# Forgetting attention with an MLP on one core: the first batch's decay columns, its attention, its waits and its loads put in another order

## The chip, the core and the metric

The kernel runs on one core of one Trainium2 chip. The metric is the device time of one execution in microseconds (us); three runs of the kernel before gave 365.26, 366.35 and 366.67 us, a median of 366.35 us.

## What is computed

There are 8 batches of 8 heads, 576 positions and 64 dimensions. Each head's scores are q·k/8, plus a decay: the difference of the running sums of log f at the two positions. Positions after one's own are masked. The attention output, 4608 rows of 512, goes through an MLP without biases.

```python
scores = scale * np.matmul(q, k.transpose(0, 1, 3, 2))
log_f = np.log(np.clip(f, 0.0001, 1.0))
cum = np.cumsum(log_f, axis=-1)
decay = cum[:, :, :, None] - cum[:, :, None, :]
scores = np.where(causal, -1000000000.0, scores + decay)
attn = np.exp(scores - np.max(scores, axis=-1, keepdims=True))
x = (attn / (attn.sum(-1, keepdims=True) + 1e-9)) @ v     # then to (4608, 512)
h = x @ w_in                                              # 512 -> 2048
out = (h - np.tanh(h)) @ w_out                            # 2048 -> 512
```

## The kernel before

All engines run in the order in which the program emits their instructions (a manual schedule covers TensorE, VectorE, ScalarE, GpSimd and SyncE), so an instruction that waits holds up everything behind it on its own engine. The order of the first batch is written out by hand at the end of the function; from the second batch on, `slot(p, take)` goes through pairs of heads and mixes `take` MLP steps into each pair's attention.

**The decay** enters the score matmul as extra contraction rows: besides the 64 dimensions, the transposed q and k have three rows that hold the running sum of log f (scaled) in a high and a low half-precision part. For the first batch these values are written as *columns* D to D+2 of `qa` and `ka`, the untransposed q and k (five blocks of up to 128 positions), before TensorE transposes them. `decay_sum` (L148) makes the running sum `cum` in two pieces, positions 0 to 255 and 256 to 575. `decay_turn` (L166) turns it by TensorE into PSUM, and `decay_cols(ib)` (L175 to L178) writes block ib's columns with three VectorE instructions. For later batches the values come as *rows*: `decay_rows` (L152 to L155) writes `chi`, `cq` and `clo`, and `load_aug` (L143 to L145) copies a batch's rows with three DMAs of SyncE's queue.

**The first batch, block by block.** `trans0(ib, what, pool, eng)` (L267) makes eight TensorE transposes of q's or k's block ib; one VectorE copy (L272) or ScalarE copy (L270) takes them into `QT` or `KT`. `scores0(ib, ti)` (L282, mask matmuls L285) makes tile ti of the block's scores, and ScalarE's exp (L287) takes it into an `e` tile. The score tiles have two PSUM buffers. Blocks 0 to 4 have 2, 4, 6, 8 and 5 tiles, 25 in all. `values0(ib)` (L295) multiplies them with v into the PSUM tile `av`, of which there is one buffer; VectorE divides by the row sums (L300 to L302) and so reads `av` last. `turn0(ib)` (L311, copy L312) transposes the result into `XR`, the MLP's input.

**MLP steps.** `step()` emits the next entry of one long list: for each unit of 512 tokens 16 steps of `mlp1`, then 16 of `mlp2`. A step of the first unit (`mlp1` with u = 0, L396) is eight matmuls of 256 tokens: step s takes the token half s // 8 and the two hidden blocks 2 (s % 8) and 2 (s % 8) + 1. ScalarE's tanh (L384) and VectorE's add (L386) follow each step. The order by hand has eight steps in the first batch, and the second batch's four pairs take 4, 4, 3 and 3, all later ones 8.

**Spins.** `spin(n)` (L239) issues n matmuls of 512 columns that nobody reads, into a new tile of the same pool and tag as `av`.

**Loads.** GpSimd issues all loads of q, k, v, `w_in` and `w_out` in program order, as casting DMAs on one queue. In the opening these are blocks of batch 0 (`load_block` L86, 128 KB each as written), `w_in` in four quarters (`load_win` L182, 512 KB each), batch 1's q and k for heads 0 to 3 in four pieces (`load_qk` L190, 144 KB each), batch 1's v in five blocks, its q and k for heads 4 to 7 (288 KB each), and `w_out` in four quarters (L186). The four quarters of `w_in` stand between the blocks of q, k and v.

**Batch 1** starts with `trans(1, 0, ...)` of q and k (L250, copies L257 and L259) and then `scores` (L335, mask L338, exp L344) and `values` (L363) of pair 0 of batch 1.

Of the kernel before, what the change touches and what calls it, by code (L numbers as in the profile page):

```python
# [8 lines left out]
FP32 = mybir.dt.float32  # L9
FP16 = mybir.dt.float16  # L10
AF = mybir.ActivationFunctionType
ALU = mybir.AluOpType
# [10 lines left out]
def kernel(  # L23
# [10 lines left out]
    nc = tc.nc  # L34
    P = 128

    B, H, S, D = q.shape
# [46 lines left out]
    def load_block(dst, src, b, n, h0=0, h1=H):  # L84
        pn = min(P, S - n * P)
        nc.gpsimd.dma_start(out=dst[0:pn, n, h0:h1, 0:D], in_=src[b, h0:h1, n * P:n * P + pn, :].rearrange("h p d -> p h d"))  # L86

    def turn_block(dst, src, b, n):
        pn = min(P, S - n * P)
        nc.sync.dma_start_transpose(out=dst[:, :, n * P:n * P + pn], in_=src[b % 2][0:pn, n, :, :])  # L90
# [4 lines left out]
    def load_v(b, n):  # L95
        load_block(vn[b % 2], v, b, n)
# [20 lines left out]
    nc.vector.memset(ka[:, :, :, D + 2:D + 3], 1.0)  # L117
    nc.vector.memset(ones16, 1.0)
    nc.vector.memset(tri16, 0.0)
    load_block(qa, q, 0, 0)  # L120
    load_block(ka, k, 0, 0)
    nc.gpsimd.affine_select(out=id16, in_=id16, compare_op=ALU.not_equal,
                            fill=1.0, base=0, pattern=[[-1, P]], channel_multiplier=1)
    load_block(qa, q, 0, 1)
    load_block(ka, k, 0, 1)
    nc.gpsimd.affine_select(out=tri16, in_=tri16, compare_op=ALU.is_ge,
                            fill=BIG, base=0, pattern=[[1, P]], channel_multiplier=-1)
    nc.vector.memset(minus16, -1.0)
# [18 lines left out]
    def decay_sum(c0, c1):  # L147
        nc.vector.tensor_tensor_scan(out=cum[:, c0:c1], data0=ones16[0:NH, c0:c1], data1=lf[:, c0:c1],  # L148
                                     initial=cum[:, c0 - 1:c0] if c0 else 0.0, op0=ALU.mult, op1=ALU.add)

    def decay_rows():
        nc.vector.tensor_scalar_mul(out=chi, in0=cum, scalar1=inv_qscale)  # L152
        nc.vector.tensor_scalar(out=cq, in0=cum, scalar1=inv_qscale, scalar2=-SHIFT * inv_qscale,
                                op0=ALU.mult, op1=ALU.add)
        nc.vector.scalar_tensor_tensor(out=clo, in0=cum, scalar=inv_qscale, in1=chi,  # L155
                                       op0=ALU.mult, op1=ALU.subtract)

    CT = {}
    keep = cst.tile([P, NJ * H], FP32)

    def decay_turn(blocks):
        t32 = ps_tr.tile([P, UW], FP32, tag="tr", name="t32")
        for ib in blocks:
            pn = min(P, S - ib * P)
            CT[ib] = (keep if 2 in blocks else t32)[0:pn, ib * H:(ib + 1) * H]
            nc.tensor.transpose(out=t32[0:pn, ib * H:(ib + 1) * H], in_=cum[0:H, ib * P:ib * P + pn], identity=id32)  # L166
        if 2 in blocks:
            nc.vector.tensor_copy(out=keep[:, 2 * H:4 * H], in_=t32[:, 2 * H:4 * H])
            nc.vector.tensor_copy(out=keep[0:D, 4 * H:5 * H], in_=t32[0:D, 4 * H:5 * H])

    def decay_cols(ib):
        ct = CT.pop(ib)
        pn = min(P, S - ib * P)
        hi = ka[0:pn, ib, :, D]
        nc.vector.tensor_scalar(out=qa[0:pn, ib, :, D + 2], in0=ct, scalar1=inv_qscale,  # L175
                                scalar2=-SHIFT * inv_qscale, op0=ALU.mult, op1=ALU.add)
        nc.vector.tensor_scalar_mul(out=hi, in0=ct, scalar1=inv_qscale)
        nc.vector.scalar_tensor_tensor(out=ka[0:pn, ib, :, D + 1], in0=ct, scalar=inv_qscale, in1=hi,  # L178
                                       op0=ALU.mult, op1=ALU.subtract)

    def load_win(f0, f1):
        nc.gpsimd.dma_start(out=win[:, :, f0:f1],  # L182
                            in_=moe_w_in[:, f0:f1].rearrange("(c p) f -> p c f", p=P))
# [5 lines left out]
    def load_qk(dst, src, b, h0, h1):  # L189
        nc.gpsimd.dma_start(  # L190
            out=dst[b % 2][:, h0:h1, :, :].rearrange("p h n d -> p h (n d)"),
            in_=src[b, h0:h1, :, :].rearrange("h (p n) d -> p h (n d)", n=NT6))

    load_v(0, 0)
    load_v(0, 1)
    load_block(qa, q, 0, 2)
    load_block(ka, k, 0, 2)
    load_win(0, DFF // 4)
    load_v(0, 2)
    load_block(qa, q, 0, 3)  # L200
    load_block(ka, k, 0, 3)
    load_v(0, 3)
    load_win(DFF // 4, DFF // 2)
    load_block(qa, q, 0, 4)
    load_block(ka, k, 0, 4)
    load_v(0, 4)
    load_win(DFF // 2, 3 * DFF // 4)
    load_win(3 * DFF // 4, DFF)
    for h in (0, 2):
        load_qk(qn, q, 1, h, h + 2)  # L210
        load_qk(kn, k, 1, h, h + 2)
    nc.sync.dma_start(out=QT[1][D:D + 2, :, :], in_=minus16)
    nc.sync.dma_start(out=KT[1][D + 2:D + 3, :, 0:S], in_=ones16[0:H, :])

# [21 lines left out]
    def spin(n):  # L236
        av = ps_av.tile([P, 2, 512], FP32, tag="av", name="spin")
        for _ in range(n):
            nc.tensor.matmul(out=av[:, 0, :], lhsT=ones16[:, 0:P], rhs=ones16[:, 0:UW])  # L239
# [20 lines left out]

    def trans0(ib, what, pool, eng):
        src, dst = (qa, ka)[what], (QT, KT)[what][0]
        pn = min(P, S - ib * P)
        t32 = pool.tile([P, UW], FP32, tag="tr" if pool is ps_tr else "m", name="t32")
        t16 = t32.bitcast(FP16)[0:D + 3, 0:H * pn].rearrange("p (h n) -> p h n", h=H)
        for h in range(H):
            nc.tensor.transpose(out=t16[:, h, :], in_=src[0:pn, ib, h, 0:D + 3], identity=id16[0:pn, 0:pn])  # L267
        to = dst[:, :, ib * P:ib * P + pn]
        if eng == "A":
            nc.scalar.activation(out=to, in_=t16, func=AF.Copy)  # L270
        else:
            nc.vector.tensor_copy(out=to, in_=t16)  # L272
# [115 lines left out]

    def mlp1(u, s):
        if u == 0:  # L390
            t, fp = divmod(s, NFT // 2)
            hps = ps_m.tile([P, UW], FP32, tag="m", name="hps")
            for w in range(2):
                ft = 2 * fp + w
                for ci in range(NCH):
                    nc.tensor.matmul(out=hps[:, w * SB:(w + 1) * SB], lhsT=win[:, ci, ft * P:(ft + 1) * P],  # L396
                                     rhs=XR[:, ci, t * SB:(t + 1) * SB], start=(ci == 0), stop=(ci == NCH - 1))
            gt = gate(hps)
            for w in range(2):
                for m in range(2):  # L400
                    GT[(0, 2 * fp + w, 2 * t + m)] = gt[:, w * SB + m * P:w * SB + (m + 1) * P]
            return
        hps = ps_m.tile([P, UW], FP32, tag="m", name="hps")
        t0 = u * UW % RING
        parts = [(0, t0, min(UW, RING - t0))]
        if t0 + UW > RING:
            parts.append((RING - t0, 0, t0 + UW - RING))
        for o, t, n in parts:
            for ci in range(NCH):
                nc.tensor.matmul(out=hps[:, o:o + n], lhsT=win[:, ci, s * P:(s + 1) * P],  # L410
                                 rhs=XR[:, ci, t:t + n], start=(ci == 0), stop=(ci == NCH - 1))
        gt = gate(hps)
        for m in range(UW // P):
            GT[(u, s, m)] = gt[:, m * P:(m + 1) * P]
# [44 lines left out]
    def slot(p, take):  # L459
# [7 lines left out]
                given += 1  # L467
        step(take - given)

    spin(8)  # L470
    decay_sum(0, 2 * P)
    decay_turn((0, 1))
    decay_cols(0)
    trans0(0, 0, ps_m, "V")
    trans0(0, 1, ps_m, "A")
    spin(2)
    decay_cols(1)
    trans0(1, 0, ps_m, "V")
    scores0(0, 0)
    scores0(0, 1)  # L480
    trans0(1, 1, ps_tr, "V")
    decay_sum(2 * P, S)
    spin(2)
    decay_turn((2, 3, 4))
    scores0(1, 0)
    values0(0)
    scores0(1, 1)
    scores0(1, 2)
    decay_cols(2)
    trans0(2, 0, ps_m, "V")  # L490
    turn0(0)
    scores0(1, 3)
    trans0(2, 1, ps_tr, "V")
    scores0(2, 0)
    values0(1)
    scores0(2, 1)
    scores0(2, 2)
    turn0(1)
    decay_rows()
    load_aug(1)  # L500
    step()
    scores0(2, 3)
    step()
    scores0(2, 4)
    for e in EL:
        nc.vector.memset(e, 0.0)
    nc.vector.memset(KT[1][:, :, S:PITCH], 0.0)
# [5 lines left out]
    load_qk(kn, k, 1, HH, H)  # L513
    for t in range(0, NFT, 4):
        load_wout(t, t + 4)
    decay_cols(3)
    trans0(3, 0, ps_m, "V")
    trans0(3, 1, ps_tr, "V")
    scores0(2, 5)
    scores0(3, 0)  # L520
    values0(2)
    scores0(3, 1)
    step()
    scores0(3, 2)
    turn0(2)
    step()
    scores0(3, 3)
    decay_cols(4)
    trans0(4, 0, ps_m, "V")
    trans0(4, 1, ps_tr, "V")  # L530
    scores0(3, 4)
    scores0(3, 5)
    step()
    scores0(3, 6)
    step()
    scores0(3, 7)
    scores0(4, 0)
    values0(3)
    scores0(4, 1)
    scores0(4, 2)  # L540
    turn0(3)
    step()
    scores0(4, 3)
    trans(1, 0, qn, QT, "AV")
    step()
    scores0(4, 4)
    trans(1, 0, kn, KT, "VV")
    values0(4)
    TAKE = [4, 4, 3, 3, 8]
    for p in range(NPAIR, len(pairs) + 1):  # L550
        slot(p, TAKE[p - NPAIR] if p < NPAIR + len(TAKE) else 8)
        if p == NPAIR:
# [30 lines left out]
```

## Time and profile before

| | |
|---|---|
| median of three runs | 366.35 us (365.26 to 366.67) |
| the profiled execution | 364.9 us, of it 363.2 us between first and last instruction |
| TensorE | 346.0 us busy (95%) |
| ScalarE | 223.1 us busy (61%) |
| VectorE | 193.5 us busy (53%) |
| GpSimd | 151.2 us busy (42%) |
| first score matmul of batch 1 (L335) | 44.94 us |
| first step of `mlp2` (L422) | 60.16 us |

In the rows of the profile PE is TensorE, PEld its weight loads, DVE VectorE, ACT ScalarE, POOL GpSimd and SP SyncE; SPq or POOLq stand for an engine's sequencer. A row of the timeline has the start, the duration (from the start of the first to the end of the last of the merged instructions), engine, line, operation, what is written and read, shape and count, and in brackets the idle time of the engine before it with what ended it. Matmuls are pipelined: the next one starts before the last one has ended, so the cost of a group is read from start to start.

### The profile page before, as it was taken

The page shows a single profiled execution, that of the slowest core. Times are in us where ns is not written, and L with a number is a line of the kernel's source. Part 1 is how long each engine was busy: PE and PEld are TensorE (multiplying, and loading weights), DVE is VectorE, ACT ScalarE, POOL GpSimd, SP SyncE. Part 2 cuts the span into 40 slices and gives each one's busy share as a digit, 9 for nine tenths or more (in the row PEclk, how much of TensorE's full clock was granted, in tenths as well). Part 3 has the DMA queues.
Part 4 walks back from the last instruction along what each step waited for, and adds up shares of the span by engine and source line. Part 5 has one row for each costly group of instructions (what it writes and reads, how often), then busy time and mean ns, then how long its engine had stood idle before and what let it go on. Part 6 is the DMA issues. An engine that isn't in the chain of part 4 may idle for free.

```text
span 363.2 us, 7847 instructions
## 1 busy us (share of the span) xinstructions
PE 346.0 (95%) x2989; PEld 200.9 (55%) x2989; DVE 193.5 (53%) x366; ACT 223.1 (61%) x411; POOL 151.2 (42%) x290
## 2 busy tenths in 40 slices
PE   6768799999999999999999999999999999999995
PEld 3558687555555555555556875555555554444442
DVE  5675679547982378237832773277327612712810
ACT  5436597646765686568756875687558734713621
POOL 8766433066267636764576447642222210000000
PEclk9989999999999999999999999999999999999999
DMA  9999999599959995999699969992220022011002
GB/s 95 155 196 169 200 203 138 72 110 174 117 36 159 140 159 55 156 150 142 67 148 155 147 65 134 157 151 44 76 75 18 18 74 74 2 47 69 3 30 85
DMA packets 149495, 38.70 MB, mean 107 GB/s; under 512 B 137362, under 2 KB 144850, under 8 KB 149458
## 3 DMA queue, kind: packets, MB, share of 16 engines
q0 software_dynamic: 101184, 18.36, 71.5%
q1 hardware_dynamic: 48194, 19.77, 27.9%
q8 instruction: 23, 0.38, 0.5%
q14 instruction: 14, 0.11, 0.1%
q10 hardware_dynamic: 80, 0.08, 0.1%
HBM read 36.85 MB, written 9.44 MB: 127 GB/s over the span
## 4 chain that ended last, share of the span: by engine, by line
PE 89%; DVE 5%; ACT 2%; issue 1%; DMA 1%; POOL 0%; POOLq 0%; ACTq 0%
PE ops L422 34%; PE hps L410 30%; PE ps L335 10%; PE av L363 7%; PE hps L396 3%; DMA qn<-in_q_dram 1%; DVE gt L386 1%; ACT th L384 1%; PE ps L282 1%; PE t L267 1%; ACT e L344 1%; PE t L250 1%; PE av L295 1%; DVE KT L259 1%; DVE xn L302 1%
## 5 line engine op out<-in xcount | busy, mean ns | idle before, releaser
L422 PE MATMUL ops<-wout,gt 128*128 128x512 f16 x576 | 140.4, 378 | 0.0
L386 DVE TENSOR_TENSOR gt<-hps,th 128x512 f16<-128x512 f32 x144 | 99.1, 690 | 61.7 <-ACT th L384 61.0
L344 ACT ACTIVATE e<-ps 128x512 f16<-128x512 f32 x168 | 99.4, 594 | 49.5 <-PE ps L335 38.2
L410 PE MATMUL hps<-XR,win 128*128 128x512 f16 (+1 forms) x576 | 125.7, 355 | 0.2
L384 ACT ACTIVATE th<-hps 128x512 f32<-128x512 f32 x144 | 86.0, 597 | 30.2 <-PE hps L410 23.7
L354 POOL TENSOR_SCALAR_AFFINE_SELECT e<-e 128x128 f16<-128x128 f16 x144 | 48.8, 339 | 114.9 <-ACT e L344 114.0
L422 PEld LDWEIGHTS <-gt 128*128 128x128 f16 x576 | 51.8, 97 | 52.5
L410 PEld LDWEIGHTS <-win 128*128 128x128 f16 x576 | 52.3, 97 | 44.2 <-issue 0.5
L335 PE MATMUL ps<-QT,KT 67*128 67x512 f16 (+1 forms) x336 | 70.9, 277 | 2.5 <-DVE KT L259 1.6
L335 PEld LDWEIGHTS <-KT 67*128 67x128 f16 x336 | 32.8, 98 | 35.4 <-DVE KT L259 1.9
L426 ACT ACTIVATE ost<-ops 128x512 f32<-128x512 f32 x36 | 21.5, 597 | 38.3 <-PE ops L422 38.3
L369 DVE TENSOR_SCALAR rs<-av 128x10 f32<-128x10 f32 x28 | 4.6, 164 | 68.4 <-PE av L363 68.4
L86 POOL DMA_DIRECT2D vn<-in_v_dram x40 | 34.1, 854 | 11.3 <-DMA win<-in_moe_w_in_dram 4.5
L363 PEld LDWEIGHTS <-e 128*128 128x128 f16 x784 | 28.1, 97 | 5.5
L86 POOL DMA_DIRECT2D qn<-in_q_dram x30 | 25.8, 861 | 8.3 <-PE ps L338 2.7
L363 PE MATMUL av<-vn,e 128*128 128x65 f16 x784 | 29.1, 193 | 0.0
L86 POOL DMA_DIRECT2D kn<-in_k_dram x30 | 25.8, 858 | 0.8 <-issue 0.6
L371 DVE TENSOR_TENSOR xn<-av,rs 128x640 f16<-128x640 f32 x28 | 23.1, 825 | 1.0
L287 ACT ACTIVATE e<-ps 128x512 f16<-128x512 f32 x25 | 14.3, 596 | 12.0 <-PE ps L285 10.6
L396 PE MATMUL hps<-XR,win 128*128 128x256 f16 x128 | 16.6, 272 | 0.5 <-DVE XR L312 0.5
L259 DVE COPY QT<-t 64x576 f16<-64x576 f16 x12 | 9.7, 806 | 9.0 <-PE t L250 6.7
L259 DVE COPY KT<-t 64x576 f16<-64x576 f16 x16 | 12.7, 795 | 1.1 <-PE t L250 1.0
(81 smaller groups left out, 199.7 us busy)
## 6 DMA issues: line engine op xcount, KB each, us to landing
out_dram<-ost SPq DMA_DIRECT2D x36, 256.0 KB
vn<-in_v_dram POOLq DMA_DIRECT2D x32, 128.0 KB, 5.9
qn<-in_q_dram POOLq DMA_DIRECT2D x24, 128.0 KB, 4.4
kn<-in_k_dram POOLq DMA_DIRECT2D x24, 128.0 KB, 4.6
win<-in_moe_w_in_dram POOLq DMA_DIRECT2D x4, 512.0 KB, 9.1
wout<-in_moe_w_out_dram POOLq DMA_DIRECT2D x4, 512.0 KB, 12.6
XR<-xn SPq DMA_TRANSPOSE x56
qn<-in_q_dram POOLq DMA_DIRECT2D x1, 576.0 KB, 15.3
```

Of the source, the lines that this page charges most:

```text
L86: nc.gpsimd.dma_start(out=dst[0:pn, n, h0:h1, 0:D], in_=src[b, h0:h1, n * P:n * P + pn, :].rearrange("h p d -> p h d"))
L259: nc.vector.tensor_copy(out=to, in_=of)
L335: nc.tensor.matmul(out=ps[:, col:col + n], lhsT=KT[b % 2][0:D + 3, h, j * P:(j + 1) * P], rhs=QT[b % 2][0:D + 3, h, i0:i0 + n], start=True ...
L344: nc.scalar.activation(out=e[:, lo:hi], in_=ps[:, lo:hi], func=AF.Exp, scale=qscale)
L354: nc.gpsimd.affine_select(out=view, in_=view, compare_op=ALU.is_ge, fill=0.0, base=0, pattern=pat, channel_multiplier=-1)
L363: nc.tensor.matmul(out=av[:, a, ib, :], lhsT=E.pop((b, 2 * c + a, j, ib)), rhs=vn[b % 2][:, j, 2 * c + a, 0:D + 1], start=(j == 0), stop=( ...
L371: nc.vector.tensor_tensor(out=xn.rearrange("p i (a d) -> p a i d", a=2), in0=av[:, :, :, 0:D], in1=rs.to_broadcast([P, 2, NJ, D]), op=ALU. ...
L384: nc.scalar.activation(out=th, in_=hps, func=AF.Tanh, scale=-1.0)
L386: nc.vector.tensor_tensor(out=gt, in0=hps, in1=th, op=ALU.add)
L396: nc.tensor.matmul(out=hps[:, w * SB:(w + 1) * SB], lhsT=win[:, ci, ft * P:(ft + 1) * P], rhs=XR[:, ci, t * SB:(t + 1) * SB], start=(ci == ...
L410: nc.tensor.matmul(out=hps[:, o:o + n], lhsT=win[:, ci, s * P:(s + 1) * P], rhs=XR[:, ci, t:t + n], start=(ci == 0), stop=(ci == NCH - 1))
L422: nc.tensor.matmul(out=ops, lhsT=GT[(u, ft, m)], rhs=wout[:, ft, :], start=(ft == 0), stop=(ft == NFT - 1))
```

## The change

- The second piece of `decay_sum` comes right behind block 0's columns. `decay_turn` of blocks 2, 3 and 4 comes ahead of block 1's transposes, into the same PSUM tile as blocks 0 and 1, and `decay_cols(2, NJ)` writes the columns of blocks 2, 3 and 4 at once, three instructions in all. The tile `keep` and its two copies go.
- `decay_rows` is split in two and goes ahead with `load_aug(1)` to block 0's and 1's scores.
- Block 4 has 64 positions; `load_first` and `trans0` now place it in partitions 64 to 127.
- `w_in` is loaded in two halves instead of four quarters, and both go behind all of batch 0's blocks; the second also goes behind batch 1's first four pieces of q and k. The order of `mlp1` with u = 0 becomes: four steps of token half 0, four of token half 1 with the same hidden blocks, then the same for the other hidden blocks.
- The first batch's order has one MLP step after `scores0(4, 2)` and four more behind it: five in all instead of eight. The pairs from the second batch on take 4, 4, 3, 3, 10, 9 and then 8.
- Three more spins of one matmul each stand in blocks 1 and 2.

```diff
+    def load_first(dst, src, n):
+        p0 = max(0, (n + 1) * P - S)
+        nc.gpsimd.dma_start(out=dst[p0:P, n, :, 0:D],
+                            in_=src[0, :, n * P:(n + 1) * P - p0, :].rearrange("h p d -> p h d"))
...
     def decay_turn(blocks):
-        t32 = ps_tr.tile([P, UW], FP32, tag="tr", name="t32")
+        if not CT:
+            CT.append(ps_tr.tile([P, UW], FP32, tag="tr", name="ct"))
         for ib in blocks:
...
+            t0 = min(ib * P, S - P)
+            nc.tensor.transpose(out=CT[0][:, ib * H:(ib + 1) * H], in_=cum[0:H, t0:t0 + P], identity=id32)
-        if 2 in blocks:
-            nc.vector.tensor_copy(out=keep[:, 2 * H:4 * H], in_=t32[:, 2 * H:4 * H])
-            nc.vector.tensor_copy(out=keep[0:D, 4 * H:5 * H], in_=t32[0:D, 4 * H:5 * H])
...
-            t, fp = divmod(s, NFT // 2)
+            t, fp = s // 4 % 2, s // 8 * 4 + s % 4
...
+    load_v(0, 0)
     spin(8)
     decay_sum(0, 2 * P)
     decay_turn((0, 1))
-    decay_cols(0)
+    decay_cols(0, 1)
+    decay_sum(2 * P, S)
     trans0(0, 0, ps_m, "V")
     trans0(0, 1, ps_m, "A")
+    decay_turn((2, 3, 4))
+    decay_cols(2, NJ)
+    load_first(qa, q, 2)
+    load_first(ka, k, 2)
+    load_v(0, 1)
+    load_first(qa, q, 3)
+    load_first(ka, k, 3)
+    load_v(0, 2)
+    load_v(0, 3)
+    load_first(qa, q, 4)
+    load_first(ka, k, 4)
+    load_v(0, 4)
+    load_win(0, DFF // 2)
+    for h in (0, 2):
+        load_qk(qn, q, 1, h, h + 2)
+        load_qk(kn, k, 1, h, h + 2)
+    load_win(DFF // 2, DFF)
     spin(2)
-    decay_cols(1)
+    decay_cols(1, 2)
+    decay_rows(False)
     trans0(1, 0, ps_m, "V")
     scores0(0, 0)
     scores0(0, 1)
     trans0(1, 1, ps_tr, "V")
-    decay_sum(2 * P, S)
+    decay_rows(True)
+    load_aug(1)
     spin(2)
-    decay_turn((2, 3, 4))
     scores0(1, 0)
     values0(0)
     scores0(1, 1)
+    spin(1)
+    trans0(2, 0, ps_m, "V")
     scores0(1, 2)
-    decay_cols(2)
-    trans0(2, 0, ps_m, "V")
+    trans0(2, 1, ps_tr, "V")
+    scores0(1, 3)
     turn0(0)
-    scores0(1, 3)
-    trans0(2, 1, ps_tr, "V")
+    values0(1)
+    spin(1)
     scores0(2, 0)
-    values0(1)
     scores0(2, 1)
+    spin(1)
+    trans0(3, 0, ps_m, "V")
     scores0(2, 2)
     turn0(1)
-    decay_rows()
-    load_aug(1)
-    step()
     scores0(2, 3)
-    step()
-    scores0(2, 4)
+    trans0(3, 1, ps_tr, "V")
...
-    decay_cols(3)
-    trans0(3, 0, ps_m, "V")
-    trans0(3, 1, ps_tr, "V")
+    scores0(2, 4)
     scores0(2, 5)
     scores0(3, 0)
     values0(2)
     scores0(3, 1)
-    step()
     scores0(3, 2)
+    scores0(3, 3)
     turn0(2)
-    step()
-    scores0(3, 3)
-    decay_cols(4)
     trans0(4, 0, ps_m, "V")
+    scores0(3, 4)
     trans0(4, 1, ps_tr, "V")
-    scores0(3, 4)
     scores0(3, 5)
-    step()
     scores0(3, 6)
-    step()
     scores0(3, 7)
     scores0(4, 0)
     values0(3)
     scores0(4, 1)
     scores0(4, 2)
+    step()
     turn0(3)
+    scores0(4, 3)
     step()
-    scores0(4, 3)
+    scores0(4, 4)
+    step()
+    values0(4)
     trans(1, 0, qn, QT, "AV")
     step()
-    scores0(4, 4)
     trans(1, 0, kn, KT, "VV")
-    values0(4)
-    TAKE = [4, 4, 3, 3, 8]
+    step()
+    TAKE = [4, 4, 3, 3, 10, 9]
```

## The prediction

> **What bounds the kernel now.** I read the page first, then who waited for whom up to 45 us, then the granted clock in small windows, then the timeline of the same stretch.
>
> ```profile
> PE 346.0 (95%) x2989; PEld 200.9 (55%) x2989; DVE 193.5 (53%) x366; ACT 223.1 (61%) x411; POOL 151.2 (42%) x290
> PE   6768799999999999999999999999999999999995
> PEclk9989999999999999999999999999999999999999
> ```
>
> TensorE is busy nearly throughout; its digits fall below 9 only in the first five slices of 9.1 us and in the last. It has the same useful work in both kernels, so the change is worth what it takes from or adds to the time that TensorE loses in the opening.
>
> ```profile
> engine line waited for: us in total, times, longest us
> PE ps L335 <- DVE KT L259: 1.6, 1, 1.6
> PE t L267 <- DVE kn L177: 3.0, 2, 2.4
> PE t L267 <- DVE qn L175: 1.5, 2, 1.2
> PE t L166 <- DVE cum L148: 1.2, 1, 1.2
> PE x L311 <- DVE xn L302: 1.2, 2, 0.7
> PE ps L282 <- DVE KT L272: 0.7, 1, 0.7
> PE hps L396 <- DVE XR L312: 0.5, 1, 0.5
> ```
>
> Columns: total, times, longest. From 10.5 us on (one 0.3 of the L175 row lies earlier) these sum to 3.0 + 1.6 + 1.2 + 1.2 + 1.2 + 0.7 + 0.5 = 9.4 us.
>
> ```profile
> 21.67:25.08 3.41, 1.03 (x18) 0.85 (x16) 2.35 (x11) 1.19 (x3) 1.90 (x3) 1.00 1.45 197
> 25.08:28.49 3.41, 3.41 (x47) 3.33 (x45) 1.43 (x3) 1.13 (x2) 2.03 (x3) 0.50 1.26 205
> 42.14:45.55 3.41, 1.84 (x48) 1.61 (x46) 3.27 (x7) 0.72 (x3) 2.01 (x3) 1.00 1.24 206
> ```
>
> After the window's bounds come its length and the busy time of PE, PEld, DVE, ACT, POOL, then the granted clock. The longest stall left TensorE 1.03 us of work in 3.41, and the clock then stood at 0.50 (finer windows: from 25.01 to 28.47 us): another 3.46 x 0.5 = 1.7 us lost. A window with 1.84 us of work kept the full clock. Lost in all: 11.1 us.
>
> ```profile
> 12.51 1.78 ACT L287 ACTIVATE e<-ps 128x512 f16<-128x512 f32 x3 [2.22 <-PE ps L285]
> 12.76 0.17 DVE L300 TENSOR_SCALAR rs<-av 128x8 f32<-128x8 f32 x1 [0.46 <-PE av L295]
> 13.20 0.69 DVE L302 TENSOR_TENSOR xn<-av,rs 128x512 f16<-128x512 f32 x1
> ...
> 23.86 0.27 DVE L508 MEMSET vn<- 64x256 uint32 x1
> 24.23 0.20 DVE L175 TENSOR_SCALAR qn<-keep 128x8 f16<-128x8 f32 x1
> 24.48 0.64 PE L267 MATMUL t<-id,qn 128*67 128x128 f16 x8 [2.38 <-DVE kn L177]
> 36.51 1.08 ACT L287 ACTIVATE e<-ps 128x512 f16<-128x512 f32 x2
> 44.94 0.39 PE L335 MATMUL ps<-QT,KT 67*128 67x512 f16 x1 [1.57 <-DVE KT L259]
> ```
>
> The transposes of block 3 wait 2.38 us for its decay columns (L175), which VectorE reaches only behind an MLP add and the memsets (L508 is one). ScalarE's exps come 0.54 to 0.59 us apart when nothing holds them. Batch 1 starts at 44.94, behind VectorE's copies.
>
> ```profile
> 9.10 0.80 POOL L182 DMA_DIRECT2D win<-in_moe_w_in_dram  x1
> 17.08 0.68 POOL L86 DMA_DIRECT2D vn<-in_v_dram  x1 [1.55 <-DMA win<-in_moe_w_in_dram]
> 23.17 0.63 POOL L190 DMA_DIRECT2D qn<-in_q_dram  x1 [1.86 <-DMA win<-in_moe_w_in_dram]
> ```
>
> GpSimd's 17th load waited for the landing of its 9th (the first quarter of w_in, issued at 9.10), its 22nd for the 14th (the second): at most eight are in flight.
>
> **Prices.** Start to start, from rows of this trace: a block's eight transposes 0.48 us, its copy 0.69 and 0.67 behind their start; a score tile 0.30 to 0.35, its exp 0.2 behind; values 0.0305 a matmul (32 in 0.98, L295 at 36.5); VectorE after values 1.13 (12.76 to 13.89); an MLP step 0.87; a spin 0.22.
>
> **Decay and rows, up to block 1's scores.** VectorE now runs block 0's columns (5.38 to 5.88), the second running sum (0.87, to 6.75), the first QT copy (to 7.4), columns of blocks 2 to 4, columns of block 1, chi and cq (0.74, from 19.48 to 20.22). No row has three instructions on 128x24; on 128x8 one takes 0.12 to 0.36, three 0.5 pipelined. I take 0.5, at most 1.1. That ends at 9.2; block 1's two copies end at 9.9 and 11.0 (10.8 before). What goes between them and the scores is the running sum and its transposes: `scores0(1, 0)` starts at 11.06 instead of 11.95. clo (0.74) then ends at 11.8, before values need VectorE; `load_aug`'s three DMAs go out at 9 to 13 on an SP queue that has nothing else, needed first at 38. The 0.17 and 0.15 of the copies to `keep` are off the path. Block 4's transposes at other partitions: the row at 32.53 (64 rows) has 0.30; I take the same, 0.48 at most.
>
> **The spins are a wait of their own.** `av` has one buffer, so a spin behind `values0` must wait until VectorE has divided, and behind it in TensorE's order are the transposes and scores that feed ScalarE. The trace of before has no such case (its spins follow spins): between nothing and the whole 1.0 + 1.3 us; I take the whole, since the buffer is the same. values0(0) ends at 11.84, VectorE at 13.0; block 2's transposes go at 13.25 (12.0 without the wait), its copies end at 14.6 and 15.4. Block 1's last exp ends at 15.7, values0(1) at 16.35, VectorE at 17.5; block 2's scores start at 17.7.
>
> **Blocks 2 to 4 without MLP steps are paced by the exps.** Block 2's six: last one ends at 22.1 (block 3's copies, 20.0 and 21.4, in between). values0(2) takes 24 x 0.0305 = 0.73 to 22.85, and delays the next exp to 23.35; from there 0.54 each, so block 3's last ends at 27.7; values0(3) to 28.7. The memsets now lie at 21.4 to 22.6, ahead of VectorE's next work at 23.0, and hide there; were that cover gone, 1.2 us. Two tiles of block 4, first step at 29.3, `scores0(4, 3)` 30.4, step, `scores0(4, 4)`, step to 32.7. The exp of (4, 4) sits behind the second step's tanh and ends at 32.85; values0(4) 32.9 to 34.1, transposes and two steps to 36.4. Batch 1's scores wait for VectorE: division to 35.35, half of QT 0.81 to 36.2, an add 0.69 to 36.9, two halves of KT 0.80 each: **38.5 instead of 44.94**.
>
> **The sum.** 44.94 - 38.5 = 6.4 us earlier, with three steps fewer done, 3 x 0.87 = 2.6: gain 3.8. The other way round: from 10.6 us on my walk leaves TensorE without useful work for 0.45 (until 11.06), 1.0 + 0.55 + 1.3 (the spins' waits and an exp between them), 1.95 (eight short waits for exps), 2.1 (KT copies) and 0.65 (the three new spins), 8.0 in all against 11.1: gain 3.1. The two ways differ by the ends of matmuls, which rows overlap; I take 3.5, the middle. The steps moved into pairs of batch 2 (10 and 9) cost their 0.87 there and nothing else: from 80 to 100 us PE is busy 19.9 of 20.
>
> **Loads.** Blocks are issued 0.9 us apart and land 4.4 later (q of block 1: 3.54 to 7.95), from 6.5 on: q2 10.9 (needed 13.25), k4 about 18 (25.2), v4 19. If GpSimd had to wait for the columns of blocks 2 to 4 (8.05), all this is 1.5 later and still in time. The first half of w_in, 1049 KB at the 205 GB/s of the windows around 25 us, is issued 16th, behind the landing of the 8th load at 13, and lands at 24 to 27 (the last two quarters took 3.75 and 3.16 each); needed 29.3. Batch 1's first pieces 27 to 30 (34.1), the second half 32 to 35 (step nine, 44). From there the queue has carried the same bytes in both kernels; q and k of heads 4 to 7 land by 40.5, needed at 38.5 + 6.6 = 45.1. All hidden; with 2 to 5 us to spare, each us beyond that is a us lost.
>
> **Rivals.**
>
> *One fall of the clock (14%).* In my walk 14.1 to 17.5 holds 1.8 us of work in 3.4 and 35.1 to 38.5 holds 1.4; the trace's limit lies between 1.03 and 1.84. One fall costs up to 1.7 us: gain 1.8, 364.5 us. The Trainium skill ("TensorE: Matmul & The Clock Gate", Part 1) has the clock halved after a wholly idle window of about 3.4 us. By that rule nothing falls here, as my longest gap is 2.1; but the trace shows a fall after a window with 1.03 us of work, and the measurement decides.
>
> *Two falls, no gain (6%).* If transposes do not count as work for the clock, my stretch from 14.1 holds only 1.05 us and the one from 35.1 only 0.85, both at or below the window that fell: 2 x 1.7 = 3.4, gain 0.1, 366.3 us. The rows of before do not decide: the window that fell held 0.5 of transposes and falls either way. The Trainium skill (the same page, Part 4) says of transposes that the full clock "doesn't engage" for them, as they don't count as busy in the same way. No run here shows it.
>
> *Falls throughout, slower (10%).* While exps set the pace, TensorE works 0.33 of every 0.54 us, 61%, not far above the 54% of the window that kept its clock. If the limit lies just there, the clock falls in every second window from 11 to 38 us, four times: 6.9 - 3.5 = 3.4 slower, 369.8 us. Two falls eat the gain, the third decides (1.7 slower). For it: long stretches without MLP steps. Against: from 8 to 21.7 us each 3.41 held 2.4 to 2.7 us of work and kept the clock.
>
> *The exps don't close up (8%).* If the 19 exps of blocks 2 to 4 come 0.73 apart instead of 0.54, through copies and divisions between them, 19 x 0.19 = 3.6: no gain, 366.4 us. For it: every block is a chain of transposes, copies, scores, exps and values. Against: three exps in 1.78 us at 12.51, in just such a stretch.
>
> *The spins don't wait (12%).* Then 1.0 + 1.3 goes: 3.5 + 2.3 = 5.8, 360.5 us. For it: the spin writes only one of `av`'s two banks and is read by nobody. Against: the division reads both banks.
>
> **Numbers.** The profiled execution took 364.9 us (span 363.2), 1.45 below the median; 364.9 - 3.5 = 361.4 for an execution like it, and 366.35 - 3.5 = 362.8 for the median, chance 50%. The range takes the forecast, most of the waitless case (360.5) and the cases without gain: 360.2 to 366.6, leaving 5% below and 15% above. A measurement can tell about 0.5%, 1.8 us, from no change. Faster by more: forecast 50, waitless 12, half of one fall 7: 0.69. Same: the other half 7, no gain 6 + 8: 0.21. Slower: 0.10.
>
> **What would show it.** The row PE t <- DVE kn gone; a spin waiting about 1 us for DVE xn, twice; first L335 near 38.5; first L396 near 29; no window at clock 0.5. Wrong if L335 comes after 42, if the clock falls twice, or if the steps wait for w_in.

## The result, and the profile after

The changed kernel takes 363.68 us (median of 18 executions, 362.62 to 365.53); the kernel before, run beside it, 367.89 us (18 executions, 364.89 to 371.25). The ratio is **0.9903, 95% interval 0.9879 to 0.9927**: 1.0% faster, some 3.6 us. Executions of one kernel differ by how long the clock stood at half, and the ratio leaves out those that are over 1.5% above the fastest of their kernel.

The profiled execution after took 363.46 us, of it 361.8 between first and last instruction; that is only 1.4 us less than the profiled execution of before. The rows of the page, in the order of those shown of before:

```profile
PE 348.7 (96%) x2992; PEld 202.3 (56%) x2992; DVE 192.7 (53%) x358; ACT 223.5 (62%) x411; POOL 150.4 (42%) x288
PE   7789799999999999999999999999999999999995
PEclk9996999999999999999999999999999999999999
```

In the third slice (18.1 to 27.1 us) TensorE's digit is 8 where before had 6, but the clock's row, at 8 in the third slice before, now falls to 6 in the fourth.

Who waited for whom up to 45 us, TensorE's rows (one of 1.9 us at the program's start, the same in both kernels, is left out):

```profile
engine line waited for: us in total, times, longest us
PE spin L223 <- DVE xn L287: 2.1, 2, 1.2
PE ps L320 <- DVE KT L243: 2.0, 1, 2.0
PE ps L267 <- ACT e L272: 1.1, 3, 0.5
PE t L252 <- DVE qn L177: 0.6, 2, 0.3
PE ps L267 <- DVE KT L257: 0.3, 1, 0.3
```

The waits for decay columns shrank from 3.0 + 1.5 us to 0.6, and what is left of them lies ahead of 8.3 us; those for the running sum and for XR are gone. In their place stand the two waits of the spins for the division (2.1 us) and a longer one for KT (2.0).

The timeline of the same stretch (start, duration, engine, line, what is written and read, idle time before and what ended it):

```profile
13.00 0.39 PE L223 MATMUL spin<-ones 128*128 128x512 f16 x1 [0.88 <-DVE xn L287]
...
15.03 0.92 PE L280 MATMUL av<-vn,e 128*128 128x65 f16 x16
...
17.18 0.39 PE L223 MATMUL spin<-ones 128*128 128x512 f16 x1 [1.22 <-DVE xn L287]
...
26.28 0.58 PE L267 MATMUL ps<-QT,KT 67*128 67x128 f16 x4 [0.33 <-ACT e L272]
27.26 1.95 PE L280 MATMUL av<-vn,e 128*128 128x65 f16 x32
...
30.04 1.89 PE L381 MATMUL hps<-XR,win 128*128 128x256 f16 x8
...
38.97 1.59 DVE L243 COPY KT<-t 64x576 f16<-64x576 f16 x2
40.61 0.39 PE L320 MATMUL ps<-QT,KT 67*128 67x512 f16 x1 [1.96 <-DVE KT L243]
```

The spins wait 0.88 and 1.22 us. The 32 matmuls of values0(3) take 1.95 us where before took 1.13, and an MLP step 1.89 instead of 1.03: TensorE runs at half clock there. Batch 1 starts at 40.61, behind VectorE's two copies of KT.

The granted clock in windows of 3.4 us (length, busy PE, PEld, DVE, ACT, POOL, then the clock):

```profile
15.55:18.97 3.42, 2.10 (x31) 1.75 (x31) 1.33 (x5) 1.14 (x3) 3.38 (x6) 1.00 1.51 151
22.40:25.82 3.42, 2.96 (x49) 2.45 (x47) 2.22 (x6) 2.47 (x5) 0.00 (x0) 1.00 1.28 206
25.82:29.23 3.41, 3.08 (x53) 2.96 (x51) 0.00 (x0) 1.98 (x4) 3.34 (x5) 0.51 1.13 210
29.23:32.65 3.42, 3.42 (x41) 2.89 (x38) 1.11 (x4) 1.68 (x3) 0.45 (x1) 0.50 1.91 172
```

The clock falls at 25.8 us and stays down until 32.7, two windows of 3.4 us (in all profiles here it changes in steps of that length). It falls behind a window in which TensorE was busy for 2.96 of 3.42 us; an earlier window with 2.10 us kept the full clock. GpSimd's queue, as the row that answers to those shown of before:

```profile
25.89 2.44 POOL L86 DMA_DIRECT2D vn<-in_v_dram  x3 [5.13 <-DMA win<-in_moe_w_in_dram]
```

It waited 5.13 us for the first half of w_in, landed at 25.9; the first MLP step stands at 30.0.

### The profile page after: what moved, and what is told of

Read it like the earlier page. It is cut to its first block, busy times and chain, and to the rows that moved or that the text cites. A ratio compares the mean times of both kernels' runs of the same rounds, so it can differ in the third digit from the quotient of the medians.

```text
span 361.8 us, 7844 instructions
## 1 busy us (share of the span) xinstructions
PE 348.7 (96%) x2992; PEld 202.3 (56%) x2992; DVE 192.7 (53%) x358; ACT 223.5 (62%) x411; POOL 150.4 (42%) x288
## 4 chain that ended last, share of the span: by engine, by line
PE 91%; DVE 4%; ACT 3%; issue 1%; ACTq 0%
PE ops L407 34%; PE hps L395 30%; PE ps L320 10%; PE av L348 7%; PE hps L381 3%; PE ps L267 2%; PE spin L223 1%; DVE KT L243 1%; PE av L280 1%; PE t L252 1%; DVE gt L371 1%; PE t L234 1%; ACT e L329 1%; ACT th L369 1%; ACT e L272 1%
## 5 line engine op out<-in xcount | busy, mean ns | idle before, releaser
L411 ACT ACTIVATE ost<-ops 128x512 f32<-128x512 f32 x36 | 21.5, 598 | 39.2 <-PE ops L407 39.2
L86 POOL DMA_DIRECT2D qn<-in_q_dram x25 | 21.2, 850 | 9.8 <-PE t L234 3.6
L86 POOL DMA_DIRECT2D kn<-in_k_dram x25 | 21.4, 855 | 1.4 <-issue 1.2
L381 PE MATMUL hps<-XR,win 128*128 128x256 f16 x128 | 17.4, 281 | 0.0
```

## The experiments

Each ratio is to the kernel before, run on the same chip in the same rounds.

### The kernel before, once more

No edit; its executions and a second profile.

> The kernel before, unchanged, for more of its executions with their clocks and a second profile. Theory A (the clock's fall is part of what separates the two medians): before's executions carry mean clocks between 0.995 and about 0.985, the longer spans at the lower clocks, since where the stall at 22 to 24.5 us lies against the chip's windows of 3.4 us decides whether one or more of them run at half clock; a profile from a run near 366 us span has at least 6.8 us at clock 0.50. Rival B (the clock is the same in all, other things spread the times): all spans come at clock 0.995 and the spread of 365 to 371 us is somewhere else.

Measured: 1.002 (0.9984 to 1.0056), spans from 363.4 to 369.5 us. The second profile has a span of 369.5 us at a mean clock of 0.966; four of its windows, with the same columns as above:

```profile
13.50:17.00 3.50, 3.07 (x30) 2.80 (x29) 1.89 (x6) 1.35 (x3) 2.29 (x4) 0.50 1.98 164
20.50:24.00 3.50, 2.93 (x19) 2.21 (x19) 1.85 (x5) 1.01 (x3) 1.16 (x3) 0.50 1.67 183
27.50:31.00 3.50, 2.59 (x25) 2.59 (x25) 2.29 (x8) 0.00 (x0) 1.76 (x3) 0.50 1.55 189
51.00:54.20 3.20, 3.20 (x21) 2.34 (x19) 1.49 (x2) 2.36 (x5) 3.20 (x5) 0.50 1.59 192
```

The clock is at half from 13.3 to 33.8 us and again from 50.8 to 54.2, seven windows in all. Theory A holds. Over all 66 executions of before that were recorded with their clock in these experiments, span goes with mean clock:

| mean clock | executions | median span, us |
|---|---|---|
| 0.999 | 2 | 362.2 |
| 0.995 | 11 | 363.5 |
| 0.989 to 0.991 | 24 | 364.8 |
| 0.984 to 0.986 | 17 | 366.4 |
| below 0.983 | 12 | 368.2 |

A window of 3.4 us at half clock lowers the mean clock by 3.4 x 0.5 / 363 = 0.005, so the rows are no, one, two, three and more than three windows, and from one row to the next the span grows by 1.3 to 1.8 us. The profile from which the prediction was made, at 0.995, belongs to the best fifth. The changed kernel's 18 executions have one window (5 of them, 360.9 to 361.2 us) or two (13 of them, median 362.3), never more.

### The changed kernel without its three spins

```diff
     scores0(1, 1)
-    spin(1)
...
     values0(1)
-    spin(1)
...
     scores0(2, 1)
-    spin(1)
```

> The changed kernel without its three new single spins. Theory A (the prediction's price): the two waits of 1.0 and 1.2 us on the division go, with 0.65 us of spins, so batch 1's first scores come 1.5 to 2.9 us earlier at the same clock, and the median falls by 1.5 to 2.9 us against the changed kernel (about 0.983 of before). Rival B (the spins carry the clock): without them a window between 12 and 19 us falls to half clock, an extra 3.4 us at 0.50, and the time is the changed kernel's or up to 2 us longer (0.990 to 0.996).

Measured: 0.9822 (0.9778 to 0.9867), median 360.94 us; spans of 357.4 to 357.9 at one half-clock window, 359.1 to 359.8 at two. TensorE's waits, and then its timeline (values0(1), values0(2), the first MLP step, batch 1's start):

```profile
PE ps L320 <- DVE KT L243: 2.0, 1, 2.0
PE ps L267 <- ACT e L272: 1.1, 3, 0.5
```

```profile
13.69 0.92 PE L280 MATMUL av<-vn,e 128*128 128x65 f16 x16
18.36 0.88 PE L280 MATMUL av<-vn,e 128*128 128x65 f16 x24
25.50 1.04 PE L381 MATMUL hps<-XR,win 128*128 128x256 f16 x8
34.84 0.39 PE L320 MATMUL ps<-QT,KT 67*128 67x512 f16 x1 [1.97 <-DVE KT L243]
```

Theory A holds: 0.9903 - 0.9822 = 0.8%, or 3.0 us; at one window the spans are 360.9 to 361.2 against 357.4 to 357.9. The spins cost about what their waits and their own time cost (2.1 + 0.65), and saved no window: both kernels have one or two. Without them values0(2) starts at 18.4 instead of 21.4.

### The same spins in buffers that nobody reads

```diff
+    def spin_m(n):
+        sm = ps_m.tile([P, UW], FP32, tag="m", name="spinm")
+        for _ in range(n):
+            nc.tensor.matmul(out=sm, lhsT=ones16[:, 0:P], rhs=ones16[:, 0:UW])
...
-    spin(1)
+    spin_m(1)
...
```

> The changed kernel with the same three spins, each into a buffer of the pool of the MLP (three buffers) instead of the one of av, so that they wait for no division. Theory A: the two waits go, the clock stays as in the changed kernel: 1.5 to 2.3 us faster than it (about 0.985 of before). Rival B (the waits only hid what comes next): the transposes behind the spins run earlier, but ScalarE's exps, 0.54 to 0.60 us apart, set the end; less than 0.5 us.

Measured: 0.9827 (0.9783 to 0.9872), as without spins. Theory A holds, and the run splits the price: the wait for `av`'s buffer is nearly all of it. What the 0.65 us of matmuls cost doesn't show in the ratios; at equal clock the spans are some 0.4 us longer than without spins (358.0 against 357.7 at one window, 359.9 against 359.5 at two), from two to four executions each.

### Six spins in the stretch where the clock fell

```diff
     scores0(3, 2)
+    spin_m(1)
     scores0(3, 3)
+    spin_m(1)
     scores0(3, 4)
+    spin_m(1)
...
     scores0(3, 7)
+    spin_m(1)
```

> The changed kernel with six more single spins, one behind each of the tiles 2 to 7 of block 3, in free buffers: 1.3 us more of unread matmuls in the stretch from 22.4 to 27 us that ends in 6.9 us of half clock in the profile. Theory A (too little work, as the clock counts it, lets it fall): no fall at 25.8, mean clock 0.999, batch 1's first scores at 38 to 39 us instead of 40.6, 1.5 to 3 us faster than the changed kernel. Rival B (the fall has another cause, or exps pace that stretch so that the clock costs nothing there): mean clock still 0.989 or the time within 0.5 us, or 1.3 us slower by the spins.

Measured: 0.9873 (0.9832 to 0.9915); mean clock 0.999 in two executions of six, 0.994 to 0.995 in the others, against 0.988 to 0.994 of the changed kernel. The profile's windows over the stretch, and batch 1's start:

```profile
19.60:23.00 3.40, 3.07 (x58) 2.60 (x57) 2.53 (x11) 2.69 (x6) 1.18 (x2) 1.00 1.13 203
23.00:26.40 3.40, 3.19 (x44) 2.39 (x44) 1.58 (x4) 2.29 (x5) 2.69 (x4) 1.00 1.28 208
26.40:29.80 3.40, 3.37 (x76) 2.94 (x75) 1.06 (x3) 2.64 (x6) 1.12 (x2) 1.00 1.12 212
```

```profile
38.24 0.39 PE L325 MATMUL ps<-QT,KT 67*128 67x512 f16 x1 [1.98 <-DVE KT L248]
```

Theory A holds in direction: the fall at 25.8 is gone, and batch 1 starts at 38.24 us. The size is below what A gave: 1.1 us by the ratios (0.9903 - 0.9873). Four of the six executions still lose one window (in this profile from 39.2 to 42.7 us, behind the wait for KT).

### The decay part alone

The decay columns, rows and block 4's place as changed; TensorE's order, eight steps, loads and the pairs' steps as before:

```diff
-    decay_cols(0)
+    decay_cols(0, 1)
+    decay_sum(2 * P, S)
     trans0(0, 0, ps_m, "V")
     trans0(0, 1, ps_m, "A")
+    decay_turn((2, 3, 4))
+    decay_cols(2, NJ)
...
+    decay_rows(False)
...
+    decay_rows(True)
+    load_aug(1)
...
-    decay_cols(2)
...
-    decay_cols(3)
...
-    decay_cols(4)
```

> Only the decay part of the change: columns of blocks 2 to 4, rows and block 4's place as changed; the order of TensorE's work, the eight MLP steps, the loads and the pairs' steps as before. Theory A (the waits for the columns are most of the gain): the waits of 2.4, 1.2 and 1.2 us go, batch 1's first scores come at about 41 us instead of 44.9 at one window of half clock, and the windows at half clock become fewer (mean clock 0.990 or above in most runs): 3 to 5 us faster than before, that is as fast as the whole change. Rival B (the stall only moves to the exps, which share ScalarE with the MLP's tanh, and to later loads): under 1 us at equal clock.

Measured: **0.9824** (0.978 to 0.9869), median 360.26 us, mean clock 0.998 to 1.0 in five of six executions. The timeline at block 3 and at batch 1's start:

```profile
23.59 0.34 PE L267 MATMUL ps<-QT,KT 67*128 67x128 f16 x3 [1.57 <-DVE QT L257]
...
40.32 0.39 PE L320 MATMUL ps<-QT,KT 67*128 67x512 f16 x1 [1.57 <-DVE KT L243]
```

Theory A holds, with more than it gave: 6.4 us by the ratio, where 3 to 5 were expected, so this part alone is faster than the whole change by 0.8%. Batch 1 starts 4.6 us earlier than in the first profile, with all eight steps done. Of the 2.4 us stall 1.57 is left, now for VectorE's copy behind the memsets, yet five of six executions kept the clock through it.

### The changed kernel with the loads of before

The order of GpSimd's loads as before, w_in in quarters between the blocks; all else as changed.

```diff
-    load_first(qa, q, 2)
...
-    load_win(DFF // 2, DFF)
+    load_v(0, 1)
+    load_first(qa, q, 2)
+    load_first(ka, k, 2)
+    load_win(0, DFF // 4)
+    load_v(0, 2)
+    load_first(qa, q, 3)
+    load_first(ka, k, 3)
+    load_v(0, 3)
+    load_win(DFF // 4, DFF // 2)
...
+    load_win(3 * DFF // 4, DFF)
...
```

> The changed kernel with its loads in the order of before (w_in in quarters between the blocks). Theory A (the prediction's: loads are hidden, since q and k of block 3 land at about 19 and 20 us in that order and are needed at 18.2 and 19.5): 0 to 1 us slower than the changed kernel. Rival B (the order of loads is needed for the rest of the change): block 3's and 4's transposes wait 1 to 3 us more, and the clock falls in a further window: 2 to 4 us slower, the time of before.

Measured: 0.9916 (0.9883 to 0.995), beside 0.9903. Theory A holds: beside the spins' waits the order of the loads is worth 0.5 us by the ratios, which lies within the intervals; in the profile TensorE waits 0.48 us for q of block 3.

### No spins, and the loads of before

Both edits above together: the three `spin(1)` taken out, and the loads as in the last diff.

> The changed kernel without the three spins and with the loads in the order of before. Theory A (without the spins' waits, TensorE comes to block 3's transposes at 15 us, but q and k of block 3 land at 19 to 20 us in that order): a wait of 3 to 4 us on those loads, 2 to 4 us slower than without spins and with the new loads (0.988 to 0.993 of before). Rival B (something else paces blocks 2 and 3): within 1 us of it (0.982 to 0.985).

Measured: 0.9964 (0.9923 to 1.0006), median 367.17 us, mean clock down to 0.970. Block 3's transposes:

```profile
18.98 1.07 PE L252 MATMUL t<-id,qn 128*67 128x128 f16 x8 [3.28 <-DMA qn<-in_q_dram]
```

Theory A holds for the wait's place and size, but the price is higher: 0.9964 - 0.9822 is 5.2 us. At equal clock it is 3.2 to 3.5 us, the wait itself (at one window 361.2 against 357.4 to 357.9, at two 362.4 to 362.8 against 359.1 to 359.8). The rest is half clock: in this profile the clock falls at 18.5 us, within the wait, and stays down until 35.6, and nine of the twelve executions have a mean clock of 0.985 or less, the kernel without spins none. The new order of loads, worth next to nothing beside the spins, carries the kernel without them.

### The kernel before with spins in its stalls

```diff
     decay_cols(3)
+    spin(10)
     trans0(3, 0, ps_m, "V")
...
     decay_cols(4)
+    spin(5)
     trans0(4, 0, ps_m, "V")
```

> The kernel before with ten spins ahead of block 3's transposes and five ahead of block 4's, where TensorE waits 2.4 and 1.2 us for the decay columns; the waits stay. Theory A (a large part of before's time is the half clock that the stall sets off, one to six windows of 3.4 us by the execution): mean clock 0.995 or above in nearly all executions, spans of 361.5 to 363.5 us, the median 3 to 4 us below before's, with the waits still there. Rival B (the stall itself is the cost): the median falls by less than 1.5 us and the spread of before stays.

Measured: 0.9988 (0.9948 to 1.0028), which tells no difference. The medians of all twelve and of all 23 executions of before are 364.23 and 366.70 us; seven of twelve ran at clock 1.0, with spans of 362.2 to 362.5, one at 0.995, and four at 0.979 to 0.991, with spans up to 366.9. The spins fill the stall in the profile:

```profile
21.94 2.32 PE L239 MATMUL spin<-ones 128*128 128x512 f16 x10
...
24.41 0.64 PE L267 MATMUL t<-id,qn 128*67 128x128 f16 x8
```

The run doesn't decide between the theories: eight of twelve executions at 0.995 or above is less than A's "nearly all", and the medians differ by 2.5 us where A gave 3 to 4 and B under 1.5. What it does show is the level without any fall: 362.2 to 362.5 us with the stall's length kept, against 358.5 to 358.6 for four of the decay part's executions at 0.998 to 1.0. So the waits that the decay part takes away are worth some 3.8 us by themselves, and the clock is the rest of its 6.4.

### Batch 1's transposes earlier, with attention ahead and without

On the changed kernel without spins, and then on the decay part alone:

```diff
     scores0(4, 3)
     step()
+    trans(1, 0, qn, QT, "AV")
     scores0(4, 4)
     step()
-    values0(4)
-    trans(1, 0, qn, QT, "AV")
-    step()
     trans(1, 0, kn, KT, "VV")
+    values0(4)
+    step()
     step()
```

```diff
+    trans(1, 0, qn, QT, "AV")
     turn0(3)
     step()
     scores0(4, 3)
-    trans(1, 0, qn, QT, "AV")
-    step()
-    scores0(4, 4)
     trans(1, 0, kn, KT, "VV")
+    scores0(4, 4)
+    step()
     values0(4)
```

> The changed kernel without the three spins, and with the transposes of batch 1's q and k (pair 0) two and one steps earlier, ahead of values0(4). Theory A: VectorE's copies of KT are done before TensorE reaches batch 1's scores, the wait of 2.0 us there goes, and with it the half-clock window behind it (1.7 us): 2 to 3.5 us faster than without spins alone, about 0.974 of before. Rival B (batch 1's first pieces of q and k land too late for it, or VectorE is the limit there whatever the order): under 0.7 us.

> The decay part alone, with batch 1's first transposes three emissions earlier, ahead of a step and of scores0(4, 4). Theory A (attention ahead of the MLP steps brings nothing of its own once the columns are ahead; only the wait at batch 1's start is left to take): 1 to 2 us faster than the decay part alone and the same within 0.5 us as the changed kernel without spins with early transposes (0.973). Rival B (attention ahead does bring 1 to 2 us there): 0.977 to 0.982 of before.

Measured: 0.9732 (0.9689 to 0.9775) with attention ahead, mean clock 0.994 to 1.0; 0.9824 (0.9785 to 0.9862) on the decay part alone. In the first, TensorE no longer waits at batch 1's start:

```profile
33.26 0.38 PE L320 MATMUL ps<-QT,KT 67*128 67x512 f16 x1
```

Theory A holds for the first, 3.3 us. On the decay part alone the earlier transposes bring nothing by the ratio, as the ratio was 0.9824 without them too; that is nearest to rival B. Here the clock hides a gain: four of its six executions lose a window, where five of the decay part's six lost none, and at a mean clock of 1.0 the spans are 357.0 to 357.1 against 358.5. With attention ahead they are 355.0 to 355.6 at 0.998 to 1.0, so attention ahead of the MLP steps, with the new loads, is worth about 1.7 us at equal clock, once the spins and the wait at batch 1 are out of the way.

### The best version

The same without spins and with early transposes, and with four free spins in block 3:

```diff
     scores0(3, 4)
+    spin_m(1)
...
     scores0(3, 7)
+    spin_m(1)
```

Tiles 5 and 6 have one each as well.

> The same with four single spins behind tiles 4 to 7 of block 3, in free buffers. Theory A (the clock still falls in the exp-paced stretch without them): mean clock 0.999 and up to 1.5 us faster than the kernel without them. Rival B (the clock stands there anyway): 0 to 0.9 us slower, the time of the spins.

Measured: **0.9715** (0.9675 to 0.9756), median 356.78 us (356.58 to 357.26), mean clock 0.999 or 1.0 in all six executions; 2% under the changed kernel. Theory A holds for the clock. The gain in time over the kernel without these four spins, 0.5 us in medians, is within both intervals; the spread of the executions is 0.7 us instead of 2.3.

## Why the prediction was right, and where it was not

**The forecast held, in part by luck**: 3.5 us less and 362.8 us, range 360.2 to 366.6, were forecast; measured are 363.68 us and a ratio that makes 3.6 us. The two profiled executions, from which the forecast's sum can be checked, differ by 1.4 us only; why the medians differ by more stands below, at the step that failed.

**The walk held.** `scores0(1, 0)` was put at 11.06 and its second matmul stands at 11.06 (its first could start on the earlier copy, at 10.55); block 2's transposes 13.25, measured 13.22; its scores 17.7, measured 17.40. From 25.8 on the clock spoils the comparison, and the kernel with six free spins restores it: values0(3) at 27.36 (27.7 forecast), the first MLP step at 28.90 (29.3), batch 1 at 38.24 us (38.5).

**The spins' wait was taken at the right end** of its bounds: 0.88 + 1.22 us measured, 1.0 + 1.3 taken. The rival "the spins don't wait" fell with the first profile; its price, 5.8 - 3.5 = 2.3 us, was 2.8 by free buffers (0.9903 - 0.9827) and 3.0 without spins.

**The loads were hidden**: the first half of `w_in` landed at 25.9 us (24 to 27 forecast) for a step at 30.0, and no row of TensorE's waits names a load. Three instructions on 128x24 took 0.65 us from first start to last end, against 0.5 taken.

**The exps closed up**: after 17.9 us of the profile exps that wait for nothing come 0.5 to 0.6 us apart; that rival fell too.

**The step that failed is the clock, twice.** First, "the trace's limit lies between 1.03 and 1.84" us of TensorE's busy time in a window: the window ahead of the fall here held 2.96, one with 2.10 kept the clock. Busy time in the rows is not what the clock goes by. The forecast's "no window at clock 0.5" was wrong in all 18 executions, and "one fall" was the case that came in the profile, at twice its length: batch 1 came 2.1 us later than forecast. Nor did it come in either of the two stretches named there, but behind 22.4 to 25.8 us, where exps set the pace, the stretch of the rival "falls throughout". (The fall of before, read as 25.01 to 28.47 us, lies at 25.08 to 28.49; that is the same 1.7 us.)

The sum of the prediction shows the size of it. From 10.5 us to batch 1 the profile after has 5.5 us without work on TensorE (the exps' waits are 1.1, where 1.95 and 0.55 were put down), 0.65 of spins, and 6.8 x 0.5 = 3.4 of half clock: 9.6 us lost where 8.0 were forecast, 11.1 before. That makes 1.5 us of gain, as the two profiles have it.

Second, the kernel before was taken at the 1.7 us that its one profile showed; 53 of its 66 executions lose two or more such windows. The two errors lie on opposite sides and nearly cancelled; that 3.6 came so close to 3.5 is luck. At one window each, the spans are 363.5 and 360.9, a gain of 2.6 us; what is left of the measured 3.6 comes from windows that the changed kernel no longer loses.

**Which part brought it.** Of the 11.1 us that the prediction listed as lost, 3.0 + 1.2 + 1.2 us were waits for columns and running sum and 1.7 the clock. The decay part alone measured 6.4 us by its ratio. So the part that works is the decay part; the spins took 3 us back; attention ahead and the loads together add nothing by the ratios (0.9822 against 0.9824 without them). That last is the clock again: at a mean clock of 0.994 the spans are 357.4 to 357.9 with them and 360.7 without, but with them every execution loses one or two windows, and without them five of six lose none. The halves of w_in and the order of the first unit's steps were not tried each by itself.

**What the clock goes by stays open.** The Trainium skill ("TensorE: Matmul & The Clock Gate", Part 1) has the clock halved after an idle window of about 3.4 us; here it fell behind a window busy for 2.96 of 3.42 us. The length that the Trainium skill gives for a window fits: 6.8 us for two. The rule on transposes in Part 4 of the same page of the Trainium skill would lower that window's count, but leaving transposes out doesn't put the windows in order either. That window has 0.91 us of transposes of q and k and 0.38 of XR's, so some 1.7 us of other work, and the clock fell; in the decay part alone the window from 20.45 to 23.86 us (laid back in steps of 3.413 us from the clock's fall at the end of that trace, 358.4 us) is busy for 1.83 us, 1.06 of it transposes, so 0.8 of other work, and the clock stood. No run here changed transposes alone. Six matmuls of 512 columns in the stretch that fell did keep the clock up.

## What to carry to other kernels

Write small operands that a later stage waits for as soon as their inputs exist, for all blocks at once: here the decay part alone, with three early VectorE instructions for the columns of three blocks, measured 6.4 us, more than the whole change. A filler matmul needs a buffer of its own; put into a buffer whose last reader is another engine, it is a wait that holds up everything behind it (here 2.1 us in two places). Look at several executions before taking a clock's fall as a fixed cost.

## What the runs showed of the hardware that was not expected

The same program loses no or up to seven windows of half clock by the execution: before's spans go from 362.1 to 369.6 us as its mean clock goes from 0.999 to 0.966. A wait of 3.3 us came with 17 us at half clock in one profile, a wait of 1.57 us with none in another. Where a wait lies against the windows of 3.4 us matters: the wait of 2.0 us for KT lies inside one window in five profiles (TensorE busy for 1.44 to 1.46 us of it), and the clock fell behind it in all five; in the changed kernel's profile the same wait is shared by two windows (busy for 2.56 and 2.24), and the clock stood. Busy time alone doesn't decide it: windows with 1.84 us kept the clock in the first profile of before and in the decay part's, and one with 1.85 lost it in the second profile of before. And a stretch in which TensorE was busy 87% of the time, with small score matmuls and transposes, set off a fall that six unread matmuls of 512 columns took away.
